# One ring of eight places for both weight streams, in TensorE's order

## The chip, the cores and the metric

The kernel runs on one core of a Trainium2 chip. A core has TensorE (PE, matrix products), VectorE (DVE), ScalarE (ACT), GpSimd (POOL) and SyncE (SP), each with an instruction queue of its own that is worked off in order, and DMA engines that move data between the memory outside (DRAM) and the core's own storage (SBUF). TensorE writes its sums into eight banks of PSUM. The metric is device time in microseconds of one execution; less is better.

## The reference

Attention over pooled keys and values, and then a two-layer network with a gate, all in float32:

```python
B, H, S, D = 8, 8, 576, 64;  pool = 8
k_p = k.reshape(B, H, S // pool, pool, D).mean(axis=3)     # 72 pooled keys
v_p = v.reshape(B, H, S // pool, pool, D).mean(axis=3)
scores = q @ k_p.transpose(0, 1, 3, 2) / sqrt(D)
attn = softmax(scores)
x = (attn @ v_p).transpose(0, 2, 1, 3).reshape(4608, 512)
h = x @ w_in                                               # 512 x 2048
g = h * clip(h + 3, 0, 6) / 6
out = g @ w_out                                            # 2048 x 512
```

## The kernel before

**Precision.** A product of float32 numbers is made of three products of shorter ones: each operand is split into a high and a low part, and high by high, high by low and low by high are summed in PSUM. So every weight chunk holds both parts.

**Blocks and super-blocks.** The 4608 tokens are worked in 12 blocks. Blocks 0 to 3 are computed plainly, with all weights in SBUF (pools `consts`, line 144): `Step.h` (line 818) makes h for one of the 16 slices of 128 hidden columns, `Step.out` (line 849) adds its part of the output. Meanwhile the weights of the later part are prepared: `sums_of` (line 909) forms sums of weight quarters and stores them to DRAM (`wd`, line 924), `plain_of` stores the quarters and the second weights as they are. Blocks 4 to 11 are worked in pairs as four super-blocks (`super_block`, line 1001). The first product uses a scheme of seven products in place of eight (`PERIOD`, line 38, and the list `N1`): 8 pairs of slices by 7 products are 56 products of 6 matmuls each (line 1049). Then comes the second product: 16 slices `f` by 6 tiles of 128 tokens by 3 matmuls (line 1095). The attention of the next two blocks is spread in small steps between these matmuls by `Paced`, whose `slot` is called at each product and each tile of tokens.

**The two streams of weights.** In a super-block the weights come from DRAM. Two products share one chunk of 512 KB: 28 chunks `wd` for the first product. Each slice of the second product has one chunk of 512 KB: 16 chunks `w2d`. So 44 chunks for each super-block, 176 in all. `next_w` (line 940) gives the chunk of a product and issues loads up to three chunks ahead into a ring `ws` of four places in the pool `late0`; it is called first by `swap` (line 1313) during block 3. `next_w2` (line 947) does the same for the second product, three ahead, into four places `ws2` in the pool `late1`; its first four loads are traced near the end of the first product of super-block 0 (line 1046). `late0` takes the storage of the first half of `consts`, free in the middle of block 3. `late1` takes the storage of the second half and of the early pools, free at the end of block 3; a tile there waits for the old tiles that it overlaps.

**Other loads.** `load_q` (line 219), `load_k` (line 232), `load_v` and `load_vr` (lines 261 and 265) bring queries, keys and values, into two places for queries and a ring of four places (`ring`, line 154) that keys, values and some other tiles share. They are issued by SyncE, as the chunks are, and a load whose place isn't free holds SyncE's queue.

**What sets the order.** The program is written as a sequence, and a planner then writes each engine's order: it runs a model of the time and takes, for each engine, the earliest written instruction that the model holds ready. The order for the first part, to step 3 of block 1, is written out by hand (`ORDER`, line 46). Behind that only two helpers fix anything: `mark` (line 166) remembers an engine's last written instruction, and `after_mark` (line 169) puts the present one behind the one remembered for its engine, without a semaphore. `next_w` calls `mark`; `next_w2` calls `after_mark`. The loads of queries, keys and values call neither, so the planner may set them ahead of chunks that are written earlier.

Of the kernel before, what the change touches and what calls it, by code (L numbers as in the profile page):

```python
# [8 lines left out]
F32 = mybir.dt.float32  # L9
F32R = mybir.dt.float32r  # L10
# [7 lines left out]
P = 128  # L18
# [18 lines left out]

PERIOD = ((1, 0), (2, 0), (7, 1), (5, 0), (6, 0), (4, 1), (3, 0))
RAW = {1: (0, 0), 2: (0, 1), 4: (1, 1)}
CHUNK, NSTREAM, AHEAD, NC, NREL = 2, 4, 3, 6, 3  # L40
TAIL = 5
WSCALE = 2.0**8
GSCALE = WSCALE**-2
# [46 lines left out]
def attention_moe_kernel(  # L90
# [19 lines left out]
    nc = tc.nc  # L110
    NB, _, NPAIR, S = q.shape
    SP = S // POOL
    NT, DM = out.shape
    NF = w_in.shape[0]
# [10 lines left out]
    for j, t in enumerate(starts):  # L125
        end, mine = t + BLOCKS[j], []
        while t < end:
            n = min(end, (t // S + 1) * S, t + (256 if j == 0 else end)) - t
# [40 lines left out]
    def after_mark():  # L169

        if len(window) == 2 and traced[-1].engine in marks:
            behind(traced[-1], marks[traced[-1].engine])
# [46 lines left out]
    def load_q(tile):  # L219

        qtiles[tile] = []
        for i, (b, s0, n, _) in enumerate(tile):
            t = pool.tile([P, NPAIR, P], F32, name="qt", bufs=2) if i == 0 else ring("qt")
            t = t if i == 0 else t[:, : NPAIR * P].rearrange("p (c t) -> p c t", c=NPAIR)
            if n < P:
                nc.gpsimd.memset(t[:, :, P // 2 :] if i == 0 else t[:, :, : P // 2], 0.0)
            nc.sync.dma_start(t[:, :, i * (P // 2) : i * (P // 2) + n], q[b, :, :, s0 : s0 + n])
            qtiles[tile].append(t)

    kraw = {}  # L230

    def load_k(b, p):
        kraw[b, p] = ring("kst")
        nc.sync.dma_start(kraw[b, p], k[b, p])

    ksum = {}

# [23 lines left out]
    def load_v(b, p):  # L261
        vraw[b, p] = ring("vst")
        nc.sync.dma_start(vraw[b, p][:, : POOL * D], v[b, p])

    def load_vr(b, g):
        vraw[b, NPAIR + g] = ring("vst")
        for c in range(3):
            nc.sync.dma_start(vraw[b, NPAIR + g][c * REM : (c + 1) * REM, : POOL * D], vr[b, g])


    pieces = {}
# [624 lines left out]
    NPR = NF // 2  # L896
    N1 = [(i, o) for t in range(NPR + 1) for o, d in PERIOD for i in [t - d] if 0 <= i < NPR]
    supers = range(PLAIN, len(BLOCKS), 2)
# [36 lines left out]
            store(w2_dram[f], w_of[f, 1].bitcast(F32))  # L935

    late = []
    loaded, loaded2 = {}, {}

    def next_w(n):  # L940
        while (m := len(loaded)) <= n // CHUNK + AHEAD and m < len(supers) * len(w_dram):
            loaded[m] = late[0].tile([P, CHUNK, 2, 2 * P], F32R, name="ws", bufs=NSTREAM)
            nc.sync.dma_start(loaded[m].bitcast(F32), w_dram[m % len(w_dram)])
            mark()
        return loaded[n // CHUNK][:, n % CHUNK]

    def next_w2(n):
        while (m := len(loaded2)) <= n + 3 and m < len(supers) * NF:
            loaded2[m] = late[1].tile([P, 2, DM], F32R, name="ws2", bufs=4)
            nc.sync.dma_start(loaded2[m].bitcast(F32), w2_dram[m % NF])  # L950
            after_mark()
        return loaded2[n]

    x_op = {}

# [45 lines left out]
    def super_block(n, j, first_att, second_att):  # L1001

        ops = dict(x_op)
        att_banks[:] = ["a0", "a1", "o3"]
        g_of, chain, parts = {}, {}, {}
        paced = Paced(first_att, len(N1) - 2)

        def bank(names, i, width=HALF):
            return psum.tile([P, DM], F32, name="psx", tag=names[i % len(names)])[:, :width]

        def gate(src, i, k):

            r = late[1].tile([P, DM], F32, name="r", tag="ro", bufs=NREL)[:, :HALF]
            nc.scalar.activation(r, src, AF.Relu, bias=half_low, scale=GSCALE / (6.0 * WSCALE))  # L1014
            nc.vector.scalar_tensor_tensor(  # L1015
                out=g_of[i][:, k], in0=r, scalar=GSCALE, in1=src, op0=ALU.min, op1=ALU.mult
            )
            mark()

        def plus(i, k, ps, kept):  # L1020
            nc.vector.tensor_tensor(out=g_of[i][:, k], in0=ps, in1=kept, op=ALU.add)  # L1021
            gate(g_of[i][:, k], i, k)

        def keep(ps):
            c = late[1].tile([P, HALF], F32, name="c", bufs=NC)
            nc.scalar.copy(c, ps)  # L1026
            return c

        def split_g(f):
            g = g_of[f // 2][:, f % 2 :: 2]  # L1030
            hi, lo = (late[1].tile([P, 2, HALF], F32R, name=m, bufs=3) for m in ("ghi2", "glo2"))
            nc.scalar.copy(hi, g)  # L1032
            nc.vector.tensor_tensor(out=lo, in0=g, in1=hi.bitcast(F32), op=ALU.subtract)  # L1033
            mark()
            parts[f] = [t.rearrange("p h t -> p (h t)") for t in (hi, lo)]

        for m, (i, o) in enumerate(N1):
            if o == 1:
                g_of[i] = late[1].tile([P, 4, HALF], F32, name=f"g{i}")
                chain[i] = [bank(["h0", "h1", "o0"], i), bank(["o1"], i), bank(["o2"], i), {}]  # L1040
            X, Y, Z, kept = chain[i]
            ps = {1: X, 2: Z, 3: Y, 4: X, 5: Y, 6: X, 7: X}[o]
            w, t = next_w(n * len(N1) + m), ops[o]
            paced.slot()
            if n == 0 and i == NPR - 2 and o == 1:
                next_w2(0)
            for c in range(2):
                for k, (l, r) in enumerate(((0, 0), (0, 1), (1, 0))):
                    nc.tensor.matmul(  # L1049
                        ps,  # L1050
                        w[:, l, c * P : (c + 1) * P],
                        t[:, r, c],
                        start=o in (1, 2, 5) and c == 0 and k == 0,
                        stop=c == 1 and k == 2,
                        skip_group_check=True,
                    )
            if o in (1, 5, 6):
                kept[o] = keep(ps)
            elif o == 2:
                plus(i, 0, ps, kept[1])  # L1060
            elif o == 3:
                plus(i, 2, ps, kept[6])
            elif o == 7:
                plus(i, 3, ps, kept[5])
            elif o == 4:
                gate(ps, i, 1)
        last_h = next(i for i in reversed(traced) if i.engine == mybir.EngineType.PE).name
        paced.upto(len(paced.steps))

        NT2 = 2 * HALF // P  # L1070
        rest = x_ops(j + 2) if j + 2 < len(BLOCKS) else []
        paced = Paced(second_att, NT2 * (NF - TAIL))
        split_g(0)
        att_banks[:] = ["a0", "a1"]
        banks = ["o0", "h0", "o2", "o1", "h1", "o3"]
        sums = {}
        for f in range(NF):
            if f + 1 < NF:
                split_g(f + 1)
            w = next_w2(n * NF + f)  # L1080
            for t in range(NT2):
                if f < NF - TAIL:
                    paced.slot()
                elif rest:
                    rest.pop(0)()
                hi, lo = (x[:, t * P : (t + 1) * P] for x in parts[f])
                products = (hi, 0), (hi, 1), (lo, 0)
                end = f == NF - 1
                if f == 0:
                    sums[t] = [(slice(0, DM), bank(banks, t, DM))]  # L1090
                    if n == len(supers) - 1 and t == NT2 - 1:
                        sums[t] = [(slice(0, 256), sums[t][0][1][:, :256]), (slice(256, 512), bank(["a0"], 0, 256))]
                for cols, pos in sums[t]:
                    for k, (l, r) in enumerate(products):
                        nc.tensor.matmul(pos, l, w[:, r, cols], start=f == 0 and k == 0, stop=end and k == 2)  # L1095
                        if f == 0 and k == 0:
                            behind(traced[-1], last_h)
                if not end:
                    continue
                tag, size = ("ro", DM) if t >= 4 else (("ghi2", "glo2")[t % 2], 2 * HALF)  # L1100
                o = late[1].tile([P, size], F32, name="o", tag=tag, bufs=3)[:, :DM]
                at = starts[j] + t * P
                for q, (cols, pos) in enumerate(sums[t]):
                    (nc.vector.tensor_copy if (t + q) % 2 else nc.scalar.copy)(o[:, cols], pos)
                    nc.sync.dma_start(out[at : at + P, cols], o[:, cols])
            if f == NF - TAIL - 1:
                paced.upto(len(paced.steps))
        assert not rest
# [204 lines left out]
    def swap():  # L1313

        consts[0].release()
        late.append(tc.alloc_tile_pool(name="late0", bufs=1, side="left", reuse_waits="tile"))
        next_w(0)

    make = [lambda i=i, h=h: sums_of(i, h) for i in range(NPR) for h in range(2)]
    plain = [lambda i=i, n=n: plain_of(i, n) for i in range(NPR) for n in range(4)]  # L1320
# [70 lines left out]
```

## Time and profile before

| | |
|---|---|
| median of 3 runs | 905.95 us (905.34 to 912.52) |
| profiled execution | 912.95 us, its span 911.2 us |
| matmuls busy | 887.9 us (97%) |
| VectorE, ScalarE busy | 572.9 us (63%), 517.1 us (57%) |
| mean granted TensorE clock | 0.996 |
| moved by DMA | 172.63 MB |

The profile is of one execution. The span runs from its first to its last instruction. Times of a view count from the start of the span, in microseconds; the mean duration of an instruction is in nanoseconds. In the groups of instructions and in the timeline, `out<-in` names the tiles written and read, x6 counts instructions, and a bracket or an arrow at the end names what ended the engine's idle time before them, and how long that was. A row of waits reads: who waited, for whom, us in total, how often, the longest. SPq is SyncE's queue, which issues DMAs. Landing is the time from a DMA's issue until all of it has arrived. In a table of stretches each row has the stretch, its length, the busy time of PE, PEld (weight loads), DVE, ACT and POOL with the number of instructions, the granted clock of TensorE (1.00 is full speed), the mean busy share of the 16 DMA engines and GB/s.

### The profile page before, as it was taken

The page shows a single profiled execution, that of the slowest core. Times are in us where ns is not written, and L with a number is a line of the kernel's source. Part 1 is how long each engine was busy: PE and PEld are TensorE (multiplying, and loading weights), DVE is VectorE, ACT ScalarE, POOL GpSimd, SP SyncE. Part 2 cuts the span into 40 slices and gives each one's busy share as a digit, 9 for nine tenths or more (in the row PEclk, how much of TensorE's full clock was granted, in tenths as well). Part 3 has the DMA queues.
Part 4 walks back from the last instruction along what each step waited for, and adds up shares of the span by engine and source line. Part 5 has one row for each costly group of instructions (what it writes and reads, how often), then busy time and mean ns, then how long its engine had stood idle before and what let it go on. Part 6 is the DMA issues. An engine that isn't in the chain of part 4 may idle for free.

```text
span 911.2 us, 14053 instructions
## 1 busy us (share of the span) xinstructions
PE 887.9 (97%) x4760; PEld 798.0 (88%) x4760; DVE 572.9 (63%) x1183; ACT 517.1 (57%) x1473; POOL 82.4 (9%) x168
## 2 busy tenths in 40 slices
PE   7899999999999999999999999999999999999998
PEld 6788888999999988988888999888998888998887
DVE  6999855578877886665636846666766444554221
ACT  5998666656666765556335755544855344544121
POOL 4100002100202010001100200100200110000000
PEclk9999999999999999999999999999999999999999
DMA  9970207985325246886645677564687433775333
GB/s 291 392 275 0 93 1 248 390 287 141 103 65 173 63 147 222 262 291 239 194 144 186 229 231 256 188 188 168 219 257 225 161 115 115 243 244 185 116 124 108
DMA packets 93527, 172.63 MB, mean 189 GB/s; under 512 B 12048, under 2 KB 50704, under 8 KB 93456
## 3 DMA queue, kind: packets, MB, share of 16 engines
q1 hardware_dynamic: 93312, 171.74, 57.2%
q8 instruction: 38, 0.62, 0.3%
q14 instruction: 33, 0.27, 0.1%
q10 hardware_dynamic: 144, 0.00, 0.0%
HBM read 139.20 MB, written 32.51 MB: 188 GB/s over the span
## 4 chain that ended last, share of the span: by engine, by line
PE 78%; DMA 8%; DVE 8%; ACT 2%; SPq 1%; issue 1%; DVEq 0%; ACTq 0%
PE psx L1095 29%; PE psx L1049 20%; PE psh L818 11%; PE pso L849 11%; DMA ws<-wd 5%; PE psa L448 3%; PE psa L624 3%; DMA stage<-q_l 2%; DMA wd<-wq 2%; PE psa L554 1%; DVE x L966 1%; ACT e L456 1%; DVE wq L915 1%; SPq L924 1%; DVE wq L920 1%
## 5 line engine op out<-in xcount | busy, mean ns | idle before, releaser
L1049 PE MATMUL psx<-x,ws 128*128 128x384 f32 x1344 | 251.1, 341 | 7.9 <-DMA ws<-wd 6.6
L1049 PEld LDWEIGHTS psx<-x,ws 128*128 128x128 f32 x1344 | 233.8, 190 | 13.6 <-DMA ws<-wd 7.7
L1095 PE MATMUL psx<-ws,ghi 128*128 128x512 f32 (+1 forms) x800 | 242.7, 384 | 0.0
L1095 PEld LDWEIGHTS psx<-ws,ghi 128*128 128x128 f32 x800 | 146.8, 188 | 27.0
L1095 PE MATMUL psx<-ws,glo 128*128 128x512 f32 (+1 forms) x400 | 153.2, 383 | 0.0
L818 PE MATMUL psh<-xhi,w 128*128 128x384 f32 (+2 forms) x520 | 145.4, 339 | 1.1 <-DVE g L830 1.0
L1033 DVE TENSOR_TENSOR glo<-g,ghi 128x768 fp32r<-128x768 f32 x64 | 63.5, 993 | 102.4 <-ACT ghi L1032 98.6
L849 PE MATMUL pso<-w,ghi 128*128 128x512 f32 x384 | 121.6, 400 | 0.0
L1032 ACT CAST ghi<-g 128x768 fp32r<-128x768 f32 x64 | 53.5, 836 | 89.9 <-PE psx L1095 87.7
L818 PEld LDWEIGHTS psh<-xhi,w 128*128 128x128 f32 x520 | 93.2, 188 | 9.2 <-DVE g L830 1.8
L456 ACT ACTIVATE e<-psa,mx 128x72 f32<-128x72 f32 x256 | 78.8, 327 | 32.8 <-DVE mx L452 31.4
L1095 PEld LDWEIGHTS psx<-ws,glo 128*128 128x128 f32 x400 | 75.2, 188 | 13.9
L818 PE MATMUL psh<-xlo,w 128*128 128x384 f32 (+2 forms) x260 | 86.8, 335 | 0.0
L1014 ACT ACTIVATE r<-g,small 128x384 f32<-128x384 f32 x96 | 55.4, 614 | 51.3 <-DVE g L1021 49.1
L484 POOL TENSOR_TENSOR a<-e,sm 128x256 f32<-128x256 f32 x60 | 39.7, 662 | 490.3 <-DVE sm L473 423.3
L1021 DVE TENSOR_TENSOR g<-psx,c 128x384 f32<-128x384 f32 x96 | 53.2, 556 | 40.5 <-PE psx L1049 39.0
L849 PEld LDWEIGHTS pso<-w,ghi 128*128 128x128 f32 x384 | 68.9, 188 | 10.3
L849 PE MATMUL pso<-w,glo 128*128 128x512 f32 x192 | 74.1, 399 | 0.0
L1026 ACT COPY c<-psx 128x384 f32<-128x384 f32 x96 | 43.2, 484 | 24.2 <-PE psx L1049 23.4
L1015 DVE SCALAR_TENSOR_TENSOR g<-r,g 128x384 f32<-128x384 f32 x96 | 51.4, 563 | 5.2 <-ACT r L1014 4.9
L826 ACT ACTIVATE g<-psh,small 128x384 f32<-128x384 f32 (+2 forms) x65 | 37.8, 581 | 29.7 <-PE psh L818 16.3
L456 ACT ACTIVATION_READ_ACCUMULATOR e<-psa,mx 128x1 f32 x256 | 54.1, 211 | 0.0
(120 smaller groups left out, 1172.5 us busy)
## 6 DMA issues: line engine op xcount, KB each, us to landing
ws<-wd SPq DMA_DIRECT2D x112, 512.0 KB, 4.3
ws<-w2d SPq DMA_DIRECT2D x64, 512.0 KB, 3.3
out<-o SPq DMA_DIRECT2D x35, 256.0 KB, 2.9
raw<-w_in_l SPq DMA_DIRECT2D x16, 512.0 KB, 8.5
raw<-w_out_l SPq DMA_DIRECT2D x16, 512.0 KB, 9.2
w2d<-w SPq DMA_DIRECT2D x16, 512.0 KB, 5.3
wd<-wq SPq DMA_DIRECT2D x64, 128.0 KB, 2.0
kst<-k_l SPq DMA_DIRECT2D x28, 288.0 KB, 3.8
```

What stands on the lines that cost most here:

```text
L456: nc.scalar.activation(self.e[:, h], self.ps[:, h], AF.Exp, bias=self.mx[:, h : h + 1], accum_out=self.sm[:, h : h + 1])
L484: engine.tensor_tensor(out=self.a[:, : 4 * D].rearrange("p (h s) -> p h s", h=4), in0=e[:, :, :D], in1=sm[:, :, None].broadcast_to([P, 4, D]),
L818: nc.tensor.matmul(self.ps, l[f][:, c, :], r[:, c, :], start=c == 0 and i == 0, stop=c == NCC - 1 and i == 2)
L849: nc.tensor.matmul(pos, l, r, start=f == 0 and i == 0, stop=f == NF - 1 and i == 2)
L1014: nc.scalar.activation(r, src, AF.Relu, bias=half_low, scale=GSCALE / (6.0 * WSCALE))
L1015: nc.vector.scalar_tensor_tensor(out=g_of[i][:, k], in0=r, scalar=GSCALE, in1=src, op0=ALU.min, op1=ALU.mult)
L1021: nc.vector.tensor_tensor(out=g_of[i][:, k], in0=ps, in1=kept, op=ALU.add)
L1026: nc.scalar.copy(c, ps)
L1032: nc.scalar.copy(hi, g)
L1033: nc.vector.tensor_tensor(out=lo, in0=g, in1=hi.bitcast(F32), op=ALU.subtract)
L1049: nc.tensor.matmul(ps, w[:, l, c * P : (c + 1) * P], t[:, r, c], start=o in (1, 2, 5) and c == 0 and k == 0, stop=c == 1 and k == 2, skip_ ...
L1095: nc.tensor.matmul(pos, l, w[:, r, cols], start=f == 0 and k == 0, stop=end and k == 2)
```

## The change

Both streams go through one ring of eight places. A list `chunks` holds the 44 chunks of a super-block in the order in which TensorE reads them, 28 of `wd` and then 16 of `w2d`, for all four super-blocks. `chunk(n)` issues loads up to seven ahead of chunk n and gives its tile. Of each eight chunks in a row, four lie in `late0` (`ws0`) and four in `late1` (`ws1`), so the storage of both pools stays what it was. As long as `late1` isn't there, only the first four chunks are loaded; chunks 4 to 7 are written at the first product of super-block 0. The extra call at line 1046 goes. Every chunk's load calls `mark`, and every load of queries, keys and values calls `after_mark`: from the first chunk on, it stands behind the last chunk written before it in SyncE's order. The tiles are flat and are viewed in the old shapes for the matmuls.

```diff
-CHUNK, NSTREAM, AHEAD, NC, NREL = 2, 4, 3, 6, 3
+CHUNK, NSTREAM, NFIRST, NC, NREL = 2, 8, 4, 6, 3
...
             nc.sync.dma_start(t[:, :, i * (P // 2) : i * (P // 2) + n], q[b, :, :, s0 : s0 + n])
+            after_mark()
...
         nc.sync.dma_start(kraw[b, p], k[b, p])
+        after_mark()
...
         nc.sync.dma_start(vraw[b, p][:, : POOL * D], v[b, p])
+        after_mark()
...
             nc.sync.dma_start(vraw[b, NPAIR + g][c * REM : (c + 1) * REM, : POOL * D], vr[b, g])
+            after_mark()
...
-    loaded, loaded2 = {}, {}
-
-    def next_w(n):
-        while (m := len(loaded)) <= n // CHUNK + AHEAD and m < len(supers) * len(w_dram):
-            loaded[m] = late[0].tile([P, CHUNK, 2, 2 * P], F32R, name="ws", bufs=NSTREAM)
-            nc.sync.dma_start(loaded[m].bitcast(F32), w_dram[m % len(w_dram)])
+    chunks = [w for _ in supers for w in (*w_dram, *w2_dram)]
+    loaded = {}
+
+    def chunk(n, ahead=NSTREAM - 1):
+
+        while (m := len(loaded)) <= n + ahead and m < len(chunks):
+            if m % NSTREAM >= NFIRST and len(late) < 2:
+                break
+            side = m % NSTREAM >= NFIRST
+            loaded[m] = late[side].tile(
+                [P, 2 * DM], F32R, name=f"ws{side}", bufs=NSTREAM - NFIRST if side else NFIRST
+            )
+            t, src = loaded[m].bitcast(F32), chunks[m]
+            if len(src.shape) == 4:
+                src = src.rearrange("p k m c -> p (k m c)")
+            else:
+                src = src.rearrange("p m c -> p (m c)")
+            nc.sync.dma_start(t, src)
             mark()
-        return loaded[n // CHUNK][:, n % CHUNK]
-
-    def next_w2(n):
-        while (m := len(loaded2)) <= n + 3 and m < len(supers) * NF:
-            loaded2[m] = late[1].tile([P, 2, DM], F32R, name="ws2", bufs=4)
-            nc.sync.dma_start(loaded2[m].bitcast(F32), w2_dram[m % NF])
-            after_mark()
-        return loaded2[n]
+        return loaded[n]
+
+    PER = len(w_dram) + len(w2_dram)
+
+    def next_w(n, m):
+        t = chunk(n * PER + m // CHUNK)
+        return t.rearrange("p (k m c) -> p k m c", k=CHUNK, m=2)[:, m % CHUNK]
+
+    def next_w2(n, f):
+        return chunk(n * PER + len(w_dram) + f).rearrange("p (m c) -> p m c", m=2)
...
-            w, t = next_w(n * len(N1) + m), ops[o]
+            w, t = next_w(n, m), ops[o]
             paced.slot()
-            if n == 0 and i == NPR - 2 and o == 1:
-                next_w2(0)
...
-            w = next_w2(n * NF + f)
+            w = next_w2(n, f)
...
-        next_w(0)
+        chunk(0)
```

## The prediction

> **What bounds the kernel now.** I read the page's busy times first, then TensorE's own waits, the granted clock by stretches, and last what SyncE's queue did before each of TensorE's longest waits.
>
> ```profile
> span 911.2 us, 14053 instructions
> PE 887.9 (97%) x4760; PEld 798.0 (88%) x4760; DVE 572.9 (63%) x1183; ACT 517.1 (57%) x1473; POOL 82.4 (9%) x168
> PE psx L1049 <- DMA ws<-wd: 6.6, 9, 1.8
> PE psx L1049 <- DVE g L1021: 1.1, 2, 0.7
> PEld psx L1049 <- DMA ws<-wd: 7.7, 12, 2.0
> ```
>
> TensorE is busy for 97% of the span, and no other engine for more than 63%. So only what lets TensorE stand still, or run slowly, can be won without removing matmuls, and the change removes none. Behind the first microseconds its largest wait is for the streamed chunks of the first product (line 1049): 9 times, 6.6 us together. The weight loads show the same stalls as 7.7 us; that is not added, since both rows tell of one queue. No wait for the chunks of the second product (line 1095) shows.
>
> The second cost is the clock. The columns that count here are the stretch, PE's busy time, and the granted clock, third from the end.
>
> ```profile
> 6.00:361.00 355.00, 345.19 (x1917) 306.75 (x1917) 275.43 (x619) 246.94 (x749) 43.85 (x87) 1.00 0.54 179
> 361.10:364.40 3.30, 3.30 (x12) 3.30 (x11) 0.90 (x1) 0.89 (x2) 0.00 (x0) 0.50 0.87 330
> 364.50:385.00 20.50, 20.50 (x120) 20.50 (x119) 14.19 (x25) 11.49 (x21) 0.00 (x0) 1.00 0.84 267
> 364.50:412.20 47.70, 44.83 (x252) 42.87 (x251) 31.88 (x59) 28.39 (x70) 0.41 (x2) 1.00 0.84 281
> 412.30:415.60 3.30, 3.30 (x14) 3.30 (x13) 1.96 (x6) 1.98 (x7) 1.54 (x4) 0.50 1.03 395
> 415.70:910.00 494.30, 487.27 (x2556) 437.72 (x2554) 261.07 (x498) 237.02 (x645) 33.28 (x62) 1.00 0.57 186
> 359.71 0.41 PE L1049 MATMUL psx<-x,ws 128*128 128x384 f32 x1 [1.84 <-DMA ws<-wd]
> 411.34 0.45 PE L1049 MATMUL psx<-x,ws 128*128 128x384 f32 x1 [1.80 <-DMA ws<-wd]
> ```
>
> Between 6 and 910 us the clock is halved in two stretches of 3.3 us, and each begins about 1 us after one of the two longest stalls (1.84 and 1.80 us) has ended; the seven shorter stalls have none behind them. Each half-rate stretch costs at most half of its 3.3 us, 1.65 us. By matmuls it is somewhat less in the first: 12 where full speed (120 in 20.5 us, 0.171 us each) needs 2.05 us, so 1.25 us.
>
> Why were the two chunks late? SyncE's queue, in the order of time:
>
> ```profile
> 331.89 0.54 SPq L227 DMA_DIRECT2D qt<-q_l  x1
> 333.08 18.27 SPq L924 DMA_DIRECT2D wd<-wq  x12
> 351.45 1.44 SPq L855 DMA_DIRECT2D out<-o  x3
> 352.94 1.05 SPq L263 DMA_DIRECT2D vst<-v_l  x2
> 354.08 0.43 SPq L943 DMA_DIRECT2D ws<-wd  x1
> 355.04 0.55 SPq L227 DMA_DIRECT2D qt<-q_l  x1
> 401.19 2.17 SPq L950 DMA_DIRECT2D ws<-w2d  x4
> 403.46 0.42 SPq L943 DMA_DIRECT2D ws<-wd  x1
> DMA to landing us min/median/max: 5.5/5.5/5.5
> DMA to landing us min/median/max: 7.8/7.8/7.8
> ```
>
> The chunk that TensorE wanted at 357.87 (359.71 less 1.84) was issued at 354.08, behind stores that held the queue until 351.45 + 1.44 us and two loads of values, and took 5.5 us (the first landing row). The one wanted at 409.54 was issued at 403.46, straight behind four chunks of the other stream, and took 7.8 us (the second). So one stall comes from the opening of the first super-block, the other from the collision of the two streams.
>
> **The change, part by part.** *One ring, seven chunks ahead instead of three.* A super-block takes 28 chunks of the first product and 16 of the second.
>
> ```profile
> 424.30:496.30 72.00, 72.00 (x347) 60.28 (x345) 37.44 (x66) 28.98 (x77) 4.29 (x8) 1.00 0.49 162
> 779.70:841.10 61.40, 59.87 (x338) 58.16 (x337) 32.28 (x59) 30.27 (x59) 0.00 (x0) 1.00 0.70 233
> DMA to landing us min/median/max: 3.1/4.3/8.7
> ```
>
> The first product of the last super-block, where nothing else runs on TensorE, takes 61.4 / 28 = 2.19 us a chunk: the old lead of three chunks is 6.6 us, the new one of seven 15.3 us. Chunks of the first stream land in 4.3 us (median) and 8.7 us (worst). So 6.6 us covers the median with 2.3 us left for the queue and not the worst; 15.3 us covers the worst with 6.6 us left. In the second product a chunk lasts 72.0 / 16 = 4.5 us, and seven are 31 us. The four-chunk burst at 401.19 goes, because these chunks now stand behind the last of the first product. I therefore take all of the 6.6 us of stalls out. Bytes and issues stay what they are (176 chunks of 512 KB), and 233 GB/s at a DMA share of 0.70 is met today in the tightest stretch, so that a longer lead needs no more bandwidth.
>
> *The half-rate stretches.* If the two long stalls go, so do the two stretches behind them: 2 x 1.65 = 3.3 us (2.5 us if both cost what the first does by matmuls). I take 3.3. [...]
>
> *Chunks 4 to 7 at the first opening.* They no longer wait for places 0 to 3, but for the storage of the second half, which block 3's weights hold until its last matmuls.
>
> ```profile
> 348.96 0.40 PE L849 MATMUL pso<-w,glo 128*128 128x512 f32 x1
> 346.50:350.00 3.50, 3.50 (x20) 3.10 (x19) 2.01 (x6) 1.97 (x4) 0.00 (x0) 1.00 0.00 0
> 346.52 0.41 PE L448 MATMUL psa<-kbd,qt 128*128 128x144 f32 x2
> DMA to landing us min/median/max: 3.2/3.2/3.2
> DMA to landing us min/median/max: 5.8/5.8/5.8
> ```
>
> Line 849 last runs at 348.96, so the four can be issued by 349.4 if the planner writes them ahead of the last stores of line 924, and while the DMA engines are idle (share 0.00 at 346.5 to 350). Behind those stores and the three outputs it is 352.9; with the 5.5 us of today's landing that is 358.4, 0.5 us late; and at worst the 1.84 us stall stays whole, with its half-rate stretch, 3.5 us. I take zero, nearer to the first case, since the median landing of 4.3 us puts even the late issue at 357.2.
>
> *Loads of q, keys and values behind the last chunk issued.* The issues of four lines on SyncE's queue are affected (227, 234, 263, 268); each is now held until the chunk seven ahead has been issued, which is when the chunk before the present one is free, that is, about where the load stands in the program. Queued behind such a waiting chunk are other loads and the outputs; who waits for those are the scores (TensorE, line 448) and the sums of keys and values (VectorE, lines 248 and 367). How far were they ahead before?
>
> ```profile
> 570.82 0.32 SPq L950 DMA_DIRECT2D ws<-w2d  x1
> 572.20 0.55 SPq L227 DMA_DIRECT2D qt<-q_l  x1
> SPq L227 <- PE psa L448: 38.1, 14, 7.9
> SPq L263 <- DVE ksum L248: 7.5, 6, 2.6
> ```
>
> Most were held by their own places: q waited 14 times for the scores to read the tile before (7.9 us at most), values for the sums of keys. The load at 572.20 already stands behind the chunk of its step. So for most the edit costs nothing; and a q load that holds the queue for 7.9 us, which used up the old lead, fits the new one. One load was far ahead: q at 331.89, landed after 3.2 us (first landing row) and read by line 448 at 346.52. In the changed kernel it stands behind chunks 4 to 7. Its cost lies between zero (the planner sets the scores later, other products fill) and the wait worked out under the slower rival; I take zero, since TensorE's order outside the first block is the planner's, and the program's own place for these scores is the fourth chunk.
>
> *The sum.* 6.6 + 3.3 = 9.9 us of the profiled execution, whose time was 912.95 us around its span of 911.2: 903.05. What is late next is VectorE's g at 1.1 us in two waits, left in. The profiled execution lies 7.0 us above the median of 905.95 (runs 905.34 to 912.52). The two long stalls with their stretches make 1.84 + 1.80 + 3.3 = 6.9 us of that. I read the quicker runs as those where the two stalls do not happen; then 9.9 - 6.9 = 3.0 us are left to win from the median: 902.9, the same floor. **Forecast: 903 us**, 0.3% under the median; its own range is 900 to 906.5.
>
> **The rivals.** I call 1% (9.06 us: 896.9 and 915.0) what a measurement here can tell from no change.
>
> *The whole gain comes off the median.* If the 7.0 us lie elsewhere (the first loads, which I can't see vary), the quicker runs have the 9.9 us too: 905.95 - 9.9 = 896.05. For it: the late issue at 354.08 has causes in program order. Against: 6.9 against 7.0 us. 0.18, of which 0.16 beyond 1%.
>
> *The opening stall stays.* Chunk 4 late by the whole 1.84 us, with its stretch: 903.05 + 3.5 = 906.5. 0.13.
>
> *The half-rate stretches stay without the stalls*: 903.05 + 3.3 = 906.35. Against: none between 6 and 361 or after 415.7 us. [...] 0.04.
>
> *Slower: the opening's q load is late and TensorE waits in order.* If line 448 keeps its place at 346.52 and the four chunks go out behind the stores (351.45), q is issued at about 351.45 + 4 x 0.43 = 353.2 and lands 5.8 us later (second landing row: the q load at 355.04), at 359.0. TensorE stands for 359.0 - 346.52 = 12.5 us, and two half-rate stretches follow: 12.5 + 3.3 = 15.8, so 918.9, slower by 1.4%. It decides from 12 us of such waits (915.0 - 903.05). For it: the DMA share of 0.00 while line 924 held SyncE shows that a queue held at its head holds everything. [...] Against it: the planner sees the late load when it writes the order. 0.11.
>
> **How the numbers follow.** Forecast 0.54, the rivals 0.18, 0.13, 0.04 and 0.11. Faster by over 1%: 0.16 plus 0.02 for a forecast that wins more, 0.18. Slower: 0.11. Within 1%: 0.71. The range takes in the first rival and the opening stall with 2 us beyond them for the planner's other order: 895 to 909. Left out are the slower rival and some 0.05 at either end.
>
> **What would show it.** Right: no wait of line 1049 for the chunks above some 0.5 us in all; the clock at 1.00 from 6 to 910 us; chunks of the second stream landing singly; runs closer together than 905.34 to 912.52. Wrong: line 448 waiting for q, or VectorE's sums for keys and values, by more than they do now; chunk 4 issued behind 353; a half-rate stretch without a stall of over 1.8 us ahead of it; or a median near 896, which would put the 7.0 us elsewhere.

## The result and the profile after

The changed kernel takes **905.03 us** (median of 20 runs, 902.84 to 906.43). The kernel before, run beside it, takes 909.95 us (20 runs, 905.34 to 914.86; the 905.95 above was the median of the first three). The ratio is 0.9946 [0.9932, 0.9959]: faster by 0.5%, which is inside the 1% that was called no change. The forecast was 903, its range 895 to 909. One more execution of the kernel before, in the experiments below, was granted a clock of 0.75 throughout, took 1093.2 us and is left out of every ratio.

The page of the changed kernel, its busy times. The lines have moved: the first product is line 1065 now, the second 1111, the scores 452.

```profile
span 903.5 us, 14091 instructions
PE 884.1 (98%) x4760; PEld 796.8 (88%) x4760; DVE 571.4 (63%) x1183; ACT 513.6 (57%) x1473; POOL 86.2 (10%) x168
```

TensorE's waits that concern the change (who waited, for whom: us in total, times, the longest):

```profile
PE psx L1065 <- DVE g L1033: 2.6, 1, 2.6
PE psx L1065 <- DVE g L1039: 2.1, 3, 0.9
PE psx L1065 <- ACT o L858: 1.0, 1, 1.0
```

From the table of stretches, almost the whole span; the granted clock stands third from the end:

```profile
8.00:904.00 896.00, 878.46 (x4733) 791.15 (x4731) 568.69 (x1179) 510.86 (x1467) 83.03 (x154) 1.00 0.57 190
```

Nine waits for chunks and 6.6 us are gone, and so are both half-rate stretches: in this execution the clock is 1.00 from 8 to 904 us. (Six of the 20 executions have a mean clock of 0.997 or 0.998; where theirs fell isn't on record.) New are one wait of 2.6 us and one of 1.0 us, and VectorE's g, line 1039, has gone from 1.1 to 2.1 us. The two new long ones lie side by side at the opening of super-block 0. The timeline of SyncE's queue there (start, duration, what is issued):

```profile
317.60 1.87 SPq L959 DMA_DIRECT2D wsFalse<-wd  x4
330.73 18.82 SPq L928 DMA_DIRECT2D wd<-wq  x12
349.66 1.42 SPq L859 DMA_DIRECT2D out<-o  x3
351.17 2.00 SPq L959 DMA_DIRECT2D wsTrue<-wd  x4
353.21 0.55 SPq L227 DMA_DIRECT2D qt<-q_l  x1
```

The landing of the first `wsTrue`, issued at 351.17 (its size, and us to landing):

```profile
wsTrue<-wd SPq DMA_DIRECT2D x1, 512.0 KB, 5.6
```

And the timeline of TensorE:

```profile
346.32 0.51 PE L1065 MATMUL psx<-x,wsFalse 128*128 128x384 f32 x2
347.86 6.51 PE L1065 MATMUL psx<-x,wsFalse 128*128 128x384 f32 x36 [1.03 <-ACT o L858]
356.95 4.24 PE L1065 MATMUL psx<-x,wsTrue 128*128 128x384 f32 x23 [2.58 <-DVE g L1033]
```

Chunk 4, the first `wsTrue`, is issued at 351.17, behind the twelve stores and the three outputs, and lands 5.6 us later, at 356.8. TensorE was ready for it at 356.95 - 2.58 = 354.37. The page names VectorE's g, which ends at about the same time; the experiment with five early places tells the two apart. And from 347.86 TensorE runs 36 matmuls of the first product without a single one of the attention between them.

What is missing there is the work of three loads of q. Before (two of them are merged into one row, the second at 331.89), and after, with the one at 353.21 above:

```profile
293.37 0.55 SPq L227 DMA_DIRECT2D qt<-q_l  x1
323.40 9.03 SPq L227 DMA_DIRECT2D qt<-q_l  x2
```

```profile
359.41 0.55 SPq L227 DMA_DIRECT2D qt<-q_l  x1
372.97 0.55 SPq L227 DMA_DIRECT2D qt<-q_l  x1
```

SyncE issues the loads of q in one and the same sequence in both kernels (36 in each trace, of the same sizes), so these are the same three: the 18th, 19th and 20th, now 60, 36 and 41 us later. The scores that read q, before and after:

```profile
322.23 1.63 PE L448 MATMUL psa<-kbd,qt 128*128 128x144 f32 x12
331.21 0.65 PE L448 MATMUL psa<-kbd,qt 128*128 128x144 f32 x4
338.74 0.66 PE L448 MATMUL psa<-kbd,qt 128*128 128x144 f32 x4
```

```profile
321.26 1.14 PE L452 MATMUL psa<-kbd,qt 128*128 128x144 f32 x8
364.33 1.14 PE L452 MATMUL psa<-kbd,qt 128*128 128x144 f32 x8
```

With two each at 346.52 and 349.89, the kernel before runs 24 score matmuls between 320 and 351 us, the changed kernel 8, and its next ones only at 364.33.

The same stretch of work in three kernels: from the first matmul of super-block 0 to its end, and from there to the last matmul. First before, then after, then the changed kernel with the loads left unordered (the next section).

```profile
343.42:496.27 152.85, 147.99 (x759) 132.70 (x757) 90.54 (x174) 77.31 (x205) 8.79 (x20) 0.98 0.66 220
496.27:907.35 411.08, 406.70 (x2159) 369.03 (x2157) 216.68 (x418) 201.22 (x545) 28.12 (x52) 1.00 0.58 188
```

```profile
340.44:491.27 150.83, 146.27 (x776) 131.78 (x774) 93.39 (x187) 80.28 (x232) 12.87 (x24) 1.00 0.65 217
491.27:899.73 408.46, 406.75 (x2159) 370.17 (x2157) 215.53 (x418) 199.15 (x545) 29.92 (x52) 1.00 0.58 193
```

```profile
342.02:486.30 144.28, 144.06 (x758) 129.93 (x757) 91.09 (x175) 76.10 (x205) 9.40 (x20) 1.00 0.69 234
486.30:894.54 408.24, 406.89 (x2159) 370.15 (x2157) 213.20 (x418) 198.77 (x545) 27.35 (x52) 1.00 0.57 189
```

Super-blocks 1 to 3 gain 2.6 us, with the loads ordered or not (411.08 to 408.46 and 408.24). Super-block 0 tells them apart: 152.85, 150.83 and 144.28. After the change it holds 776 matmuls instead of 759: attention work that had been done ahead of it was pushed into it. Against the kernel with the loads unordered it is busy for 2.2 us more (146.27 against 144.06), and TensorE stands still for 150.83 - 146.27 = 4.6 us instead of 0.2. Part of this comes back: super-block 0 starts 1.6 us earlier (340.44 against 342.02), since work that would have stood ahead of it is now inside. That size is rough: among the kernels with all loads unordered alone, this start lies anywhere from 341.12 to 342.72.

### The profile page after: what moved, and what is told of

Same layout as the page of the kernel before. It is cut to its first block, busy times and chain, and to the rows that moved or that the text cites. A ratio compares the mean times of both kernels' runs of the same rounds, so it can differ in the third digit from the quotient of the medians.

```text
span 903.5 us, 14091 instructions
## 1 busy us (share of the span) xinstructions
PE 884.1 (98%) x4760; PEld 796.8 (88%) x4760; DVE 571.4 (63%) x1183; ACT 513.6 (57%) x1473; POOL 86.2 (10%) x168
## 4 chain that ended last, share of the span: by engine, by line
PE 83%; DVE 8%; DMA 4%; ACT 2%; SPq 1%; issue 1%; DVEq 0%; ACTq 0%
PE psx L1111 29%; PE psx L1065 25%; PE psh L822 10%; PE pso L853 10%; PE psa L452 3%; PE psa L628 3%; DMA wd<-wq 2%; DMA stage<-q_l 2%; PE psa L558 1%; SPq L928 1%; DVE wq L919 1%; DVE wq L924 1%; DVE wq L926 1%; ACT e L460 1%; DVE x L984 1%
## 5 line engine op out<-in xcount | busy, mean ns | idle before, releaser
L1065 PE MATMUL psx<-x,wsFalse 128*128 128x384 f32 x672 | 130.7, 339 | 2.0 <-ACT o L858 1.0
L1065 PE MATMUL psx<-x,wsTrue 128*128 128x384 f32 x672 | 127.9, 339 | 3.8 <-DVE g L1033 2.6
L1111 PE MATMUL psx<-wsFalse,ghi 128*128 128x512 f32 (+1 forms) x400 | 123.0, 388 | 0.0
L1111 PE MATMUL psx<-wsTrue,ghi 128*128 128x512 f32 (+1 forms) x400 | 122.7, 386 | 0.0
L1065 PEld LDWEIGHTS psx<-x,wsTrue 128*128 128x128 f32 x672 | 116.8, 188 | 4.7 <-DVE g L1033 2.9
L1065 PEld LDWEIGHTS psx<-x,wsFalse 128*128 128x128 f32 x672 | 117.2, 188 | 2.9 <-ACT o L858 1.4
L1111 PEld LDWEIGHTS psx<-wsFalse,ghi 128*128 128x128 f32 x400 | 73.6, 188 | 15.0
L1111 PEld LDWEIGHTS psx<-wsTrue,ghi 128*128 128x128 f32 x400 | 73.4, 188 | 13.4
L1111 PE MATMUL psx<-wsFalse,glo 128*128 128x512 f32 (+1 forms) x200 | 77.6, 388 | 0.0
L1111 PE MATMUL psx<-wsTrue,glo 128*128 128x512 f32 (+1 forms) x200 | 76.6, 383 | 0.0
```

What stands on the lines that cost most here:

```text
L1065: nc.tensor.matmul(ps, w[:, l, c * P : (c + 1) * P], t[:, r, c], start=o in (1, 2, 5) and c == 0 and k == 0, stop=c == 1 and k == 2, skip_ ...
```

## The experiments

All ratios are against the kernel before, run beside the kernel on the same chip. The kernels were compared in three groups, in which its medians were 909.48 (23 runs), 909.45 (16) and 910.12 (17); the other kernels ran 6 times where no number stands with them. What the measurement does with no change at all is shown by the kernel before against itself:

> The kernel before, once more, for the granted clock of every run and a second profile. My theory says that its spread (905.34 to 914.86 over 20 runs) comes from the long stalls of line 1049 and the half-rate stretches that may follow: quick runs (905 to 908) have a mean clock of 0.998 to 1.000, slow ones (911 to 915) 0.996 or less, each half-rate stretch being 3.4 us at 0.5, 0.0019 of the mean; waits of line 1049 for chunks 4 to 8 us again. The rival says that the spread lies elsewhere: the clock is the same in quick and slow runs.

Measured: 909.38 (of all 12 runs) against 909.48, ratio 0.9999 [0.9982, 1.0016]. Clock and time go together, but loosely: over the 67 executions of the kernel before whose clock is on record the mean clock and the time have a correlation of -0.62, and those at 0.996 alone spread from 907.33 to 913.24 us. So the half-rate stretches are a part of the spread, and the rest isn't explained. The profile was of the execution that is left out, so that the waits for chunks were not seen a second time.

**The loads unordered.** The changed kernel without the four new `after_mark` lines behind the loads of q, keys and values.

```diff
             nc.sync.dma_start(t[:, :, i * (P // 2) : i * (P // 2) + n], q[b, :, :, s0 : s0 + n])
-            after_mark()
...
         nc.sync.dma_start(kraw[b, p], k[b, p])
-        after_mark()
...
         nc.sync.dma_start(vraw[b, p][:, : POOL * D], v[b, p])
-        after_mark()
...
             nc.sync.dma_start(vraw[b, NPAIR + g][c * REM : (c + 1) * REM, : POOL * D], vr[b, g])
-            after_mark()
```

> After, with the loads of q, keys and values free again (the four after_mark calls taken out). If the lead of seven is what helps: the same as after within 1 us (904 to 906), no chunk wait but that of the first opening. If the order of the loads is what helps: loads move ahead of chunks, chunk waits of 2 us or more come back, and the time rises by 2 to 5 us, to 907 to 910.

Measured: **900.48 us** (899.85 to 901.47), ratio 0.9897 [0.9878, 0.9916]. Neither expectation had it faster than the changed kernel. The interval lies wholly below the changed kernel's: the ordering of the loads costs 905.03 - 900.48 = 4.5 us, and the ring alone brings 9.0 us. SyncE's queue at the same place:

```profile
321.95 9.08 SPq L227 DMA_DIRECT2D qt<-q_l  x2
331.65 18.45 SPq L924 DMA_DIRECT2D wd<-wq  x12
350.19 1.43 SPq L855 DMA_DIRECT2D out<-o  x3
351.71 2.01 SPq L955 DMA_DIRECT2D wsTrue<-wd  x4
```

And TensorE:

```profile
348.49 0.41 PE L448 MATMUL psa<-kbd,qt 128*128 128x144 f32 x2
348.74 0.38 PE L554 MATMUL psa<-ident,a 128*128 128x128 f32 x2
348.95 0.27 PE L556 MATMUL psa<-ident,ar 128*128 128x128 f32 x1
349.06 0.38 PE L554 MATMUL psa<-ident,a 128*128 128x128 f32 x2
349.20 3.79 PE L1061 MATMUL psx<-x,wsFalse 128*128 128x384 f32 x18
352.82 0.38 PE L554 MATMUL psa<-ident,a 128*128 128x128 f32 x2
...
356.56 4.76 PE L1061 MATMUL psx<-x,wsTrue 128*128 128x384 f32 x26
```

Chunk 4 is issued half a microsecond *later* than in the changed kernel (351.71 against 351.17), and nobody waits for it: TensorE comes to it at 356.56, 2.2 us later than in the changed kernel (354.37). 1.6 us of that are the later start of super-block 0, with attention work done ahead of it, and scores (line 448) and transposes (554, 556) stand between the products. They can stand there since q was issued at 291.91 and from 321.95 on, ahead of the last stores. It is a near thing: the chunk landed in 4.7 us here, at 356.4; in 5.6 us, as in the changed kernel, it would have been 0.7 us late.

**The same edit in the kernel before.** Its two rings stay, and the loads get `after_mark`.

```diff
             nc.sync.dma_start(t[:, :, i * (P // 2) : i * (P // 2) + n], q[b, :, :, s0 : s0 + n])
+            after_mark()
...
         nc.sync.dma_start(kraw[b, p], k[b, p])
+        after_mark()
...
         nc.sync.dma_start(vraw[b, p][:, : POOL * D], v[b, p])
+        after_mark()
...
             nc.sync.dma_start(vraw[b, NPAIR + g][c * REM : (c + 1) * REM, : POOL * D], vr[b, g])
+            after_mark()
```

> Before, with two rings of four, and only the loads of q, keys and values set behind the last chunk. If the lead is what helps: as before within 1.5 us (ratio to before 0.9985 to 1.0015), line 1049 waits 5 to 8 us for chunks. If the loads' order is what helps: 2 us or more faster than before, and the wait at 411 us gone.

Measured: 912.16 us (910.83 to 913.35, 12 runs), ratio 1.0024 [1.0012, 1.0037]. So the ordering costs something with either arrangement of rings: 2.7 us with two (there it is behind the chunks of the first product alone, since only `next_w` calls `mark`), 4.5 us with one. Neither expectation had it slower. The waits for chunks did not get less:

```profile
PE psx L1053 <- DMA ws<-wd: 7.9, 10, 2.0
```

**Which loads?** Only the q loads unordered, and then only one of them, that of one tile of block 6.

```diff
             nc.sync.dma_start(t[:, :, i * (P // 2) : i * (P // 2) + n], q[b, :, :, s0 : s0 + n])
-            after_mark()
```

> After, with the loads of q free again and those of keys and values still behind the last chunk. If it is the loads of q that cost the 4.5 us between after and the run with all loads free: 900 to 901.5. If it is keys and values: 904 to 905.5.

```diff
-            after_mark()
+            if tile != tiles_of[6][1]:
+                after_mark()
```

> After, with one load alone set free: the q load that is written at the first product of the first super-block, my prediction's slower rival. If the loss is that the opening has no attention work to put between the products: no wait over 0.6 us between 343 and 360, and 901 to 902.5. If the loss is spread over the loads of all super-blocks: 903.5 to 905.

Measured: 901.06 us (900.74 to 903.38), ratio 0.9905 [0.9888, 0.9921], with only q unordered; 903.4 us (902.3 to 905.99), 0.9933 [0.9913, 0.9953], with one load. So the ordering of q makes nearly all of the cost, 4.0 of 4.5 us, and the one load about 1.6 of it, though the intervals of the one load and of the changed kernel overlap. The one load is the first of the three above: it is issued at 291.78 here, and the other two still late, at 357.21 and 369.24. (It is not the load of the slower rival, as the expectation says; that one, at 331.89 before, is the third.) With it alone super-block 0 has 762 matmuls and takes 147.31 us; the wait for chunk 4 stays, at 1.7 us. So one load alone isn't the cost, and keys and values make little of it. That it is these three and no later loads of q fits super-blocks 1 to 3, which lose only 0.2 us (408.46 against 408.24), but wasn't tried by itself.

**Chunk 4 early.** The changed kernel, loads ordered, with five of the eight places in the pool that is free early and three in the other.

```diff
-CHUNK, NSTREAM, NFIRST, NC, NREL = 2, 8, 4, 6, 3
+CHUNK, NSTREAM, NFIRST, NC, NREL = 2, 8, 5, 6, 3
```

> After, with five of the eight places in the storage that is free in block 3 (three in the other), so that chunk 4 is loaded with the first four. It tells what TensorE waits for 2.6 us at the opening of the first super-block of after: chunk 4, which landed at that moment, or VectorE's line 1033, which ended at that moment and is named by the profile. If it is the chunk: the wait shrinks to under 0.8 us and the time falls by about 2 us, to 902.5 to 903.5. If it is VectorE: the wait stays at 2 to 3 us, and the time at 905.

Measured: 905.14 us (904.02 to 906.98), ratio 0.9945 [0.9926, 0.9963]: no gain, where 2 us were expected. TensorE at the opening:

```profile
349.05 8.59 PE L1065 MATMUL psx<-x,wsFalse 128*128 128x384 f32 x48 [1.12 <-ACT o L858]
358.38 2.87 PE L1065 MATMUL psx<-x,wsTrue 128*128 128x384 f32 x15 [0.74 <-DMA wsTrue<-wd]
```

With chunk 4 there, TensorE runs 48 matmuls instead of 36 before it stops, and the next chunk then costs 0.74 us: so the 2.58 us were the chunk and not VectorE. But super-block 0 takes 151.02 us, no less than 150.83, for the same 776 matmuls: 0.7 us less stillness and 0.9 us more busy time, with other short waits in place of the long one. Where these come from isn't settled. So taking the wait for chunk 4 away did not win its 2.58 us back: it was not in itself the price. That it was a sign of the missing attention work fits this, and the runs with unordered loads.

With the loads unordered the same step was tried too:

> The ring of eight with unordered loads, five of its places in the pool that is free early and three in the other, so that chunk 4 no longer waits for the end of block 3. With unordered loads the profile shows no wait for chunk 4 (0.14 us at the opening), so if that wait came from the ordering of the loads alone: 900.5 us (899.5 to 901.5), no change. If the opening still loses something to the late chunks 4 to 7: 898 to 899.

901.87 us (900.93 to 902.3), 0.9906 [0.9889, 0.9923]: no gain over 900.48, if anything a loss. A wait of 1.04 us for ScalarE's exponentials at 411 is the largest that its profile has inside the super-blocks.

**Is it the lead that is written, or the places?** Chunks written three ahead of the one in use, with eight places: first with the loads ordered, then unordered.

```diff
-    def chunk(n, ahead=NSTREAM - 1):
+    def chunk(n, ahead=3):
```

> After, with the one ring and its order, but loads issued only three chunks ahead. If the lead is what helps: small chunk waits come back in the first products (3 to 5 us in all, the one behind the four-chunk burst not among them), and the time is 907 to 909. If the common order is what helps: chunk waits below 1 us beyond the opening, and 905 to 906, as after.

> One ring of eight places, the loads of q, keys and values unordered, but chunks written only three ahead of the one in use instead of seven. If the number of places is what gives the lead, because a chunk's issue goes out when its place is free and not where it stands in the program: the time of the ring of eight with free loads, 900.5 us (900 to 902), with no wait for chunks above 0.5 us in all behind the opening. If the lead written in the program counts: the ring of four's time in part, 903 to 910, with waits for chunks of 3 us or more in the first products.

Measured: 904.28 us (901.66 to 907.79), 0.9939 [0.9915, 0.9963], and 900.85 us (900.2 to 903.76), 0.9904 [0.9884, 0.9925]. Neither differs from its twin with seven ahead (905.03 and 900.48). With unordered loads the profiles agree as well: super-block 0 takes 144.45 us against 144.28, with no wait for a chunk. So the planner issues a chunk when its place is free, wherever it is written; the number of places is the lead.

In the first of the two, TensorE did once wait in order for a late q, as the slower rival had it (the profile is of its slowest execution, 907.79 us):

```profile
557.73 0.92 PE L452 MATMUL psa<-kbd,qt 128*128 128x144 f32 x4 [2.05 <-DMA qt<-q_l]
```

The stretch behind it:

```profile
558.20:561.50 3.30, 3.30 (x12) 3.11 (x11) 0.22 (x1) 0.58 (x1) 0.00 (x0) 0.50 0.56 221
```

**How many places?** One ring in TensorE's order, loads unordered, with four places in all, and with six (four and two).

```diff
-CHUNK, NSTREAM, NFIRST, NC, NREL = 2, 8, 4, 6, 3
+CHUNK, NSTREAM, NFIRST, NC, NREL = 2, 4, 4, 6, 3
```

```diff
-CHUNK, NSTREAM, NFIRST, NC, NREL = 2, 8, 4, 6, 3
+CHUNK, NSTREAM, NFIRST, NC, NREL = 2, 6, 4, 6, 3
```

> One ring for both streams in TensorE's order, all loads of q, keys and values free, but four places in all and three chunks ahead. It takes the depth away and leaves the order. If the depth is what takes the small chunk waits away: they come back, 2.5 to 6 us in all, and the time is 904 to 908. If the common order alone does it: chunk waits under 1 us and 900 to 902.

> One ring of six places (four and two), five ahead, loads unordered. Four places took 910.6 us and eight 900.5. A chunk of the first product lasts 2.19 us in the tightest stretch, so five ahead are 11.0 us, against a worst landing of 8.7 us. If the lead has to cover the worst landing and a little of the queue: 900 to 903, near the eight. If each place counts about alike: halfway, 905.5 (904 to 907).

Measured: four places 910.57 us (908.17 to 913.18, 12 runs), 1.0015 [0.9998, 1.0032], slower than either expectation; six 902.66 us (901.82 to 904.3), 0.9917 [0.9898, 0.9937]; eight 900.48. Most of it, 7.9 of 10.1 us, comes with the fifth and sixth. With six, one wait for a chunk is left, with four two that the page names and probably a third that it gives to VectorE (at 358.16, where chunk 4 is wanted):

```profile
PE psx L1061 <- DMA wsTrue<-wd: 0.7, 1, 0.7
```

```profile
PE psx L1061 <- DVE arem L577: 2.6, 1, 2.6
PE psx L1061 <- DMA wsFalse<-wd: 1.7, 2, 1.2
```

So the single order by itself brings nothing: a ring of four in that order is as slow as the two rings of four before, and a lead of three chunks is too short with one stream as with two. The waits that can be put down to chunks, 4.3 us with that third, are less than half of the 10.1 us; what makes up the rest isn't shown.

**The collision of the two streams alone.** The kernel before, with the first four chunks of the second stream written later.

```diff
-            if n == 0 and i == NPR - 2 and o == 1:
+            if n == 0 and m == len(N1) - 1:
                 next_w2(0)
```

> The kernel before with its two rings, but the first four chunks of the second stream are written at the last product of the first super-block's first product, instead of some products earlier. If the collision of the two streams makes the stall of 1.8 us at 411 (with its half-rate stretch in most executions): 909.5 - 1.8 - 1.4 = 906.3 us, and no stall there. If a lead of three chunks is short whatever stands in front: 909.5 (908.5 to 910.5), with the stall kept or moved; or the second product waits for its first chunks, 910 to 912.

Measured: 909.01 us (906.55 to 911.84, 12 runs), ratio 0.9992 [0.9974, 1.0011]: no change that can be told. The wait at 411 is gone, and 6 us later (until 417.79) the second product waits for its own first chunk, with a half-rate stretch behind it (from 419.28 on two of its matmuls take 0.85 us, the two at 418.58 took 0.46; the clock of super-block 0 is 0.99 in the mean, one stretch):

```profile
PE psx L1049 <- DMA ws<-wd: 4.2, 7, 1.5
PE psx L1095 <- DMA ws<-w2d: 1.9, 1, 1.9
```

## Why the prediction was right in its number and wrong in a step

**The stalls of line 1049, 6.6 us: right, with one exception at the opening.** With the loads unordered no wait for a chunk is left that the profile lists; six places leave 0.7 us, four leave the time of before. That seven ahead (15.3 us) cover the worst landing (8.7 us), and three (6.6 us) only the median (4.3 us), fits this; it was the storage behind it, not the written lead, that did it (three written ahead do as well).

**The half-rate stretches, 3.3 us: right.** They went with the stalls: in the profile of the changed kernel, and in that of the ring of eight with unordered loads, none is left between the opening and the last matmul of the program. In the profile of the kernel before the two lasted 3.413 us each at a clock of 0.50; one takes 0.0019 off the mean clock, so its 0.996 are two of them. Their price fits the 67 executions of the kernel before: the five that were granted 1.000 took 907.0 us in the mean, the 25 at 0.996 took 910.2, 3.2 us more. It is no more than a fit, since a stretch can also lie in the opening (in the profile with only q unordered the clock is 0.86 from 8 to 20 us, 3.4 us at half rate), where the mean clock does not tell it from the others. The rival that they stay without the stalls fell.

**The sum of 9.9 us: right for the ring,** which measured 9.0 us, or 0.9897 [0.9878, 0.9916], that is 7.6 to 11.1. This is between medians. Between the two profiled executions, for one of which the sum was made, it was more: 912.95 to 900.12, 12.8 us, of which 1.4 lie ahead of super-block 0, 8.6 in it (152.85 to 144.28) and 2.8 behind it (411.08 to 408.24). The profiled execution of the kernel before lies 3.0 us above its median, and what makes up these 3.0 isn't shown; so that the 9.0 come so near to the 9.9 is in part luck.

**The median: misread.** I took 905.95 as what the kernel takes when the two long stalls do not happen, and left 3.0 of the 9.9 us to win. Over 20 runs the median is 909.95; executions without the stretches are there, but only 5 of the 67 have a mean clock of 1.000. The 7.0 us between the profiled execution and that median were in good part the chance of three runs. The first rival (the whole gain off the median) was right on this: 909.95 - 9.9 = 900.05, and the ring alone gave 900.48. Its reason, that the 7.0 us lie in the first loads, is not shown.

**"Loads of q, keys and values behind the last chunk issued: zero": this step failed.** It measured 4.5 us. The reading ahead of it was wrong too. "One load was far ahead" were three, and the scores at 346.52 do not read the load of 331.89: a tile of queries is eight score matmuls in these traces, so the 24 between 320 and 351 are those of the loads at 283.95, 293.37 and 323.40. VectorE's waits for the loads of keys and values by `load_k`, `load_v` and `load_vr`, which I had named as a sign, did not grow (4.2 us against 7.4). I had the two ends, zero and 12.5 us with two half-rate stretches, and took the end at which the planner sets the scores later and other products fill. The first half of that happened and the second could not: the other products are those of the stream, and they run ahead of their chunks. Of super-block 0's 6.6 us more, 2.2 us are 18 matmuls of attention pushed into it from ahead of it, whose time is in good part only moved (1.6 us by the earlier start); what is lost is the stillness there, 4.6 us against 0.2: 2.58 us for chunk 4, 1.03 us for ScalarE's outputs, which hold the PSUM banks that the next products need, and 0.95 us for VectorE's g at 414. The slower rival's time for q, 353.2, was met to the hundredth (353.21) by luck: it is another load, its sum leaves out the 1.44 us of the three outputs, and its own load went out at 372.97. It had TensorE's part wrong: at the opening TensorE waited for no q, since the planner set the scores later. It can come as the rival had it: with chunks written three ahead TensorE did wait 2.05 us for a q at 557, a sixth of the 12.5.

**Chunks 4 to 7 at the opening: zero, by the wrong road.** I let them go out at 349.4, ahead of the last stores, when block 3's weights are done. They went out behind the stores and outputs, at 351.17 (I had put that case at 352.9), and the pool `late1` takes the storage in which the tiles of those very stores (`wq`) lie; which chunk overlaps which of them no run here shows. The landing of 5.6 us made chunk 4 late by 2.58 us, more than the 1.84 us that I had called the worst. Yet in the kernel with unordered loads the same issue, 0.54 us later, is in time, if only by the 0.1 us between 356.4 and 356.56. So zero is right for the ring as it ran, by little, and the lateness is mostly the ordering's: TensorE comes 2.2 us earlier with it, and the rest is the landing of 5.6 instead of 4.7 us.

**What is late next: under-counted.** VectorE's g was left in at 1.1 us and stands at 2.1 us in the changed kernel (1.5 us with five early places); with the loads unordered it is 0.7 us.

So the forecast of 903 came near, 2.0 us below the measured 905.03, through errors that cancel: a median too low by 4.0 us, 3.0 us taken off it for a ring that brings 9.5 against that median (909.95 - 900.48), and 4.5 us for the loads that were not counted: -4.0 + 6.5 - 4.5 = -2.0. Of the signs named ahead, the clock and the closer runs (3.6 us between the fastest and the slowest, against 9.5) came out; that no wait of the first product for a chunk is left did not, with the 2.58 us for chunk 4.

The version that beats both is the ring of eight without the ordering of the loads: 900.48 us, 0.9897 [0.9878, 0.9916] of before.

## What to carry to other kernels

Count how much of a stream's storage can serve the stream that is wanted now: eight places that both streams share are worth eight to each, and two rings of four only four. Before loads are put in order behind a stream, look for those that run far ahead of it, follow each to the work that reads it, and ask what work is done early because of it; a late load costs its reader's place in the order even where no one is ever seen waiting for it. And three runs whose spread is as large as the gain at stake say little about which of them is the usual one.

## What the runs showed of the hardware

**A stall of 1.84 us had half rate behind it, a longer one of 2.58 us had none.** In the profile of the kernel before the granted clock changes at 361.06, 364.47, 412.26, 415.67 and 910.60 us: two stretches of 3.413 us at 0.50, and 0.50 again behind the last matmul. From 361.06 to 412.26 it is 51.20 us, and from there to 910.60 another 498.35, which are 15.0 and 146.0 times 3.413: in this execution the changes lie on a grid of 3.413 us. In the changed kernel's profile the clock falls only at 904.90, behind the last matmul. On a grid of the same width, counted back from there, one window runs from 351.94 to 355.35 and the next to 358.76; that the grid is the same in this execution is my estimate from the one before. The windows of the grid before and behind the first stall of the kernel before, and the three at chunk 4 in the changed kernel:

```profile
357.65:361.05 3.40, 1.56 (x10) 1.37 (x9) 3.28 (x8) 1.95 (x5) 0.00 (x0) 1.00 1.06 382
361.07:364.45 3.38, 3.38 (x12) 3.38 (x11) 0.93 (x1) 0.92 (x2) 0.00 (x0) 0.50 0.88 331
```

```profile
351.95:355.34 3.39, 2.42 (x14) 2.10 (x13) 2.63 (x6) 2.25 (x5) 0.00 (x0) 1.00 1.07 281
355.36:358.75 3.39, 1.79 (x10) 1.83 (x11) 1.47 (x3) 0.99 (x3) 0.00 (x0) 1.00 0.97 390
358.78:362.15 3.37, 3.37 (x21) 3.37 (x21) 1.02 (x2) 1.59 (x3) 0.00 (x0) 1.00 1.07 384
```

The stall of 1.84 us lies in one window, and the next has a clock of 0.50. The longer one of 2.58 us is cut in two by the grid, 0.97 and 1.61 us, and the window behind it has 1.00. In these two profiles, from 8 us on and up to the last matmul, TensorE stands still for 1.7 us or more of a window four times: in the kernel before for 1.77 us (from 9.48), 1.84 us (from 357.64) and 1.80 us (from 408.84), in the changed kernel for 1.88 us (from 10.60). Behind 1.84 and 1.80 us the clock is 0.50, behind the two in the opening it is 1.00. So inside the super-blocks the stillness within one window tells the two with half rate behind them from the rest (1.84 and 1.80 against at most 1.61 us); the 1.88 us in the opening do not fit, and what else decides isn't shown. That the grid falls differently on the program in each execution would explain why, of the 67 executions of the kernel before, 5 have a mean clock of 1.000, 18 have 0.998 and 25 have 0.996; this was argued from the windows and not tried by itself.
